# Block 0's x^T handed over on the chip, and the way from projection into attention rearranged

## The chip, the cores and the metric

One core of a Trainium2 chip runs the program. The metric is the time of one execution in microseconds (us) of device time; three executions of the kernel before gave 1452.94, 1455.36 and 1454.16 us, median 1454.16. A smaller time is better.

## The reference

One transformer block over 2048 tokens of width 512, all in fp32:

```python
xn = _layernorm(x, axis=-1)          # x: 1 x 2048 x 512
s = _A_ref(xn, A_wqkv, A_wo)         # 32 heads of 16: softmax(q k^T / 4) v, then @ wo
g = _silu(_B_ref(xn, B_w_gate, B_w_up, B_w_down))   # (silu(xn wg) * (xn wu)) wd, 1792 hidden
return x + s * g
```

Attention and the feed-forward network (FFN) read the same normalised x, and meet only in the last line.

## The kernel before, in words

Numbers keep their precision by being split: a value is held as a rounded high part and the rest as a low part, and a product is three matmuls (high-high, low-high, high-low). The program has two stages.

**Projection.** Tokens go in four blocks of 512 (loop `b`, L650), and each block in twelve slots (loop `n`, L654). A slot makes one tile of 128x512 with twelve matmuls (`project`, L568): eight feature tiles (q and k, `feature_tile`, L612) and four value tiles (`value_tile`, L624). Block 0 has the value tiles first, the others last. The order of everything is written out by hand: what a slot issues stands in the loop body, each engine takes its instructions in that order, and so do the queues of SyncE (SP) and GpSimd (POOL), which issue the DMAs.

- In slots 8 to 10 the next block's x is transposed on TensorE into PSUM and split by `turn_x` (L552) into `xt[b % 2]`, two tiles of 128 x 4 x 512: ScalarE casts the high part (L558), VectorE subtracts for the low part (L561). GpSimd then stores both to DRAM, in `xt_d` (L562 to L564). `load_fx` (L147) brings them back in the FFN's layout, `fx`: 64 contraction rows, once in each half of the partitions, so that two matmuls can use the two halves of the array. The loads for block 0 are issued at slot 5 of blocks 1 and 2 (L662).
- A feature tile is split into `parts` by ScalarE (L617) and VectorE (L619) and stored by SP (L621); ScalarE squares it into `sq` (L618). `parts` comes from a pool of three buffers (`p3`), `sq` from one of five (`p5`); the `ps` tiles in PSUM have four.
- `squares` (L584) sums the squares of each head, by a matmul with a 0/1 matrix, into 32 partitions of a PSUM bank: tiles 0 to 3 in `bankx`, tiles 4 to 7 in `banky`, four matmuls side by side. `add` (L641) does this for whatever is pending, as soon as four are (L688) and at `flush` (L645), which takes the maximum over tokens.
- In block 3, the maxima over all blocks give one number `s4`, an upper bound of the scores (L708 to L719), and from it `flag`: 1 where a fixed shift is safe. `fill(3 * DC)` (L720) puts the first 24 steps of the FFN between slots 9 and 10. After slot 10's tile two matmuls with one row (L723, L724) spread `s4` over partitions and 512 columns, and ScalarE writes the shift from there (L725, to be stored in `sh_d` by GpSimd) and into the first query tile (L728).
- At slot 8 of block 3 SP issues attention's first loads: `load_k` for two tiles (twelve DMAs), `load_q` (six) and `load_v` (two).

**The handover.** `nc.values_load(flag)` (L733) reads the flag into a register of each engine; `tc.If(fast < 1)` (L734) holds a general way that this input does not take, so each engine branches across it. The last value tile's store is issued behind it (L766).

**Attention and FFN.** Loop over 32 units (L791) of eight steps: four score matmuls, ScalarE's exponential of 128x1024 (L805), value matmuls (L367). `share` (L451) puts a planned number of FFN steps into each step, so that TensorE always has work.

Of the kernel before, what the change touches and what calls it, by code (L numbers as in the profile page):

```python
# [13 lines left out]
AF = mybir.ActivationFunctionType  # L14
# [11 lines left out]
NB = 4  # L26
TB = S // NB
NT = TB // P
DT = D // P
KT = S // P  # L30
NG = H // 4
# [5 lines left out]
HALF = 64  # L37
# [13 lines left out]
def tile_block(ctx: ExitStack, tc: tile.TileContext, x, wqkv, wo, w_gate, w_up, w_down, out):  # L51
# [51 lines left out]
    def load_k(g, c, i=None):  # L103
        load_rows(kst[(g * NB + c) % RING if i is None else i],
                  k_d[:, g * 64:(g + 1) * 64, c * TB:(c + 1) * TB], KSLOT)

    def load_q(u, i=None):
        g, b = divmod(u, NB)
        load_rows(qst[u % 2 if i is None else i], q_d[:, g * 64:(g + 1) * 64, b * TB:(b + 1) * TB], QSLOT)
# [37 lines left out]
    def load_fx(b, j):  # L147
        for h in range(2):
            dst = fx[h * HALF:(h + 1) * HALF, j].bitcast(F32).rearrange("p (c u) t -> u p c t", u=2)
            for u in range(2):  # L150
                sp.dma_start(dst[u], xt_d[b, j, u * HALF:(u + 1) * HALF])
# [304 lines left out]
    with ExitStack() as pro:  # L456
        pc = pro.enter_context(tc.tile_pool(name="pc", bufs=1))
        p2 = pro.enter_context(tc.tile_pool(name="p2", bufs=2))
        p3 = pro.enter_context(tc.tile_pool(name="p3", bufs=3))
        p5 = pro.enter_context(tc.tile_pool(name="p5", bufs=5))  # L460
        plast = pro.enter_context(tc.tile_pool(name="plast", bufs=1))
        pps = pro.enter_context(tc.tile_pool(name="pps", bufs=4, space=PSUM))

# [88 lines left out]
        def turn_x(b, t, between=None):  # L552
            a = acc[t % 2]
            for c in range(DT):
                nc.tensor.transpose(a[:, c * P:(c + 1) * P], xn[t][:, c * P:(c + 1) * P], ident)
            hi, lo = (xt[b % 2][j][:, :, t * P:(t + 1) * P] for j in range(2))
            av = a.rearrange("p (c f) -> p c f", f=P)
            nc.scalar.copy(hi, av)  # L558
            if between:
                between()  # L560
            dve.tensor_sub(lo, av, hi.bitcast(F32))  # L561
            if t == NT - 1:  # L562
                for j in range(2):
                    pool.dma_start(xt_d[b, j], xt[b % 2][j].bitcast(F32))  # L564

# [46 lines left out]
        def feature_tile(b, m):  # L612
            xh, xl = xt[b % 2]
            ps = project([(wh[:, m, c], wl[:, m, c], c) for c in range(DT)], xh, xl, None)
            parts = p3.tile([P, 2, TB], F32R, tag="parts", name="parts")
            sq = p5.tile([P, TB], BF, tag="sq", name="sq")
            nc.scalar.copy(parts[:, 0], ps)  # L617
            act(sq, ps, AF.Square)  # L618
            dve.tensor_sub(parts[:, 1], ps, parts[:, 0].bitcast(F32))  # L619
            dst = (q_d if m < 4 else k_d)[:, (m % 4) * P:(m % 4 + 1) * P, b * TB:(b + 1) * TB]  # L620
            sp.dma_start(dst.rearrange("s f t -> f s t"), parts.bitcast(F32))  # L621
            return m, sq

        def value_tile(b, t):  # L624
            xh, xl = xt[b % 2]
            order = then = None
            if b == 0:
                parts = (slice(0, 2), slice(2, 3)) if t == 0 else (slice(0, 3, 2), slice(1, 2))
                order = [(i, part) for part in parts for i in range(DT)]
                then = partial(turn_x, 0, 1, partial(later, 3)) if t == 0 else None  # L630
            ps = project([(vh[:, c], vl[:, c], c) for c in range(DT)], xh, xl, slice(t * P, (t + 1) * P), order, then)
            nc.scalar.copy(vt5[:, :, t, :, :DH], ps.rearrange("p (g h d) -> p g h d", g=NG, h=4))
            if t == NT - 1:
                store = partial((pool if b < NB - 1 else sp).dma_start, v_d[:, :, b * NT:(b + 1) * NT].rearrange("g p t c -> p g t c"), vt)
                if b < NB - 1:
                    store()
                return store

        pend = []

        def add():  # L641
            while pend:
                squares(*pend.pop(0))
# [6 lines left out]
        for b in range(NB):  # L650
            more = b + 1 < NB
            slots = [(feature_tile, m) for m in range(8)]
            slots = [(value_tile, t) for t in range(NT)] + slots if b == 0 else slots + [(value_tile, t) for t in range(NT)]
            for n, (make, i) in enumerate(slots):  # L654
                if b == 0:
                    if n + 5 < 12:
                        load_w(worder[n + 5])
                    if n >= 2 and n + 2 < 12:
                        split_w(worder[n + 2], pool)
                if n == (1 if b else 2) and more:  # L660
                    load_x(b + 1)
                if b in (1, 2) and n == 5:  # L662
                    load_fx(0, b - 1)
                if b == 2 and n in (6, 7):
                    load_gu(n - 6)
                if b == 2 and n == 8:
                    load_wd(0)
                if not more and n == 2:
                    split_gu(0)
                    for bank in acc:  # L670
                        dve.memset(bank, 0.0)
                if b == NB - 1 and n == 8:
                    for c in range(2):
                        load_k(0, c)
                    load_q(0)
                    for c in range(2):
                        load_v(0, c)
                if b == 0 and n == 1:
                    rates(2, NT)
                    norm(2)  # L680
                    norm(3)
                made = make(b, i)
                if b == 0 and n == 1:
                    for t in (2, 3):
                        turn_x(0, t)
                if n == 0 and b == 1:
                    flush(0)
                elif len(pend) == 4:  # L688
                    add()
                if make is feature_tile:  # L690
                    pend.append(made)
                if b == 0 and n == 11:
                    ring(0, 2, one)
                    queries(0, one)
                if more:
                    if 2 <= n < 6:
                        stats(n - 2)
                    if n == 5:
                        rates(0, NT)
                    if 6 <= n < 10:  # L700
                        norm(n - 6)
                    if 8 <= n < 11:
                        turn_x(b + 1, n - 8)
                    if n == 10:
                        turn_x(b + 1, NT - 1)
                if n == 8 and b:
                    flush(b)
                if not more and n == 8:  # L708
                    dve.reduce_max(pk, peak, axis=AX.X)
                    dve.tensor_add(sm, pk[:, 0:1], pk[:, 1:2])  # L710
                if not more and n == 9:
                    tops = pps.tile([P, 512], F32, tag="ps", name="tops")
                    nc.tensor.transpose(tops[0:1, :P], sm, ident)
                    dve.reduce_max(s4, tops[0:1, :P], axis=AX.X)
                    dve.tensor_scalar(s4, s4, 0.51, None, op0=ALU.mult)
                    dve.tensor_scalar(flag, s4, LIMIT, None, op0=ALU.is_le)
                    dve.tensor_scalar(sel[:, :NG * NB], row[:, :NG * NB], s4, None, op0=ALU.mult)
                    for h in range(2):
                        dve.tensor_copy(selq[:, h * HALF:h * HALF + 1], s4)  # L719
                    fill(3 * DC)  # L720
                if not more and n == 10:
                    low, high = [pps.tile([P, 512], F32, tag="ps", name="low") for _ in range(2)]
                    mm(high[:2 * NG * NB], sel, row, start=True, stop=True, skip_group_check=True)  # L723
                    mm(low[:HALF + 2], selq, row, start=True, stop=True, skip_group_check=True)  # L724
                    act(shift, high[:2 * NG * NB], AF.Copy, scale=-1.0)  # L725
                    for h in range(2):
                        two_rows = slice(h * HALF, h * HALF + 2)
                        act(qst[0][two_rows], low[two_rows, None, :].to_broadcast([2, 2, 512]), AF.Copy, scale=-1.0)  # L728
                    for j in range(4):
                        pool.dma_start(sh_d[:, j * 512:(j + 1) * 512], shift.bitcast(F32))  # L730


        fast = nc.values_load(flag, min_val=0, max_val=1)  # L733
        with tc.If(fast < 1):  # L734
            with tc.tile_pool(name="gen", bufs=1) as gen:
                for h in range(2):
# [160 lines left out]
```

## Time and profile before

| what | value |
|---|---|
| median of three executions | 1454.16 us (1452.94 to 1455.36) |
| the profiled execution's own time | 1451.71 us |
| its span, first to last instruction | 1449.9 us |
| granted TensorE clock, mean | 0.998 |
| TensorE busy | 1433.2 us, 99% |
| ScalarE busy | 1094.4 us, 75% |
| VectorE busy | 539.9 us, 37% |
| first score matmul of attention | at 166.50 us |

The projection stage ends at about 165 us, so all that the change touches lies in the first ninth of the span. PE is TensorE's matmuls, PEld its weight loads, DVE VectorE, ACT ScalarE; a q behind the name (PEldq, SPq) means the engine's instruction queue, where register loads, branches and DMA issues are recorded. "x <- y" in a wait means that x stood idle until y was done.

### The profile page before, as it was taken

How to read it: one execution, taken by the hardware profiler on the slowest of the kernel's cores; microseconds unless marked ns; L12 is line 12 of the kernel's file. 1: busy time of each engine (PE TensorE's matmuls, PEld its weight loads, DVE VectorE, ACT ScalarE, POOL GpSimd, SP SyncE). 2: the span in 40 equal slices, each digit the busy share in tenths (PEclk: the TensorE clock that was granted, in tenths of full speed). 3: DMA queues.
4: the chain of work that ended last, by engine and by line, in shares of the span. 5: the costliest groups of instructions: out<-in, count | busy, mean ns of one | idle time of the engine just before them, and what ended most of it. 6: DMA issues, size and time to landing. Idle time of an engine off the chain costs nothing.

```text
span 1449.9 us, 26818 instructions
## 1 busy us (share of the span) xinstructions
PE 1433.2 (99%) x11237; PEld 804.1 (55%) x11237; DVE 539.9 (37%) x905; ACT 1094.4 (75%) x1219; POOL 89.9 (6%) x105
## 2 busy tenths in 40 slices
PE   8999999999999999999999999999999999999997
PEld 7777555555555555555555555555555555555554
DVE  6543343313423343143324431343243412424445
ACT  4433588878888888788888887888888877887774
POOL 4200200000000000000000000000000000000153
PEclk9999999999999999999999999999999999999999
DMA  8899652033264420143634311345425202315252
GB/s 267 271 288 290 160 125 71 19 76 76 66 155 105 109 71 27 40 110 78 134 75 120 87 41 34 78 102 111 122 63 125 60 21 51 78 41 169 75 205 78
DMA packets 129556, 154.92 MB, mean 107 GB/s; under 512 B 12700, under 2 KB 79260, under 8 KB 128404
## 3 DMA queue, kind: packets, MB, share of 16 engines
q1 hardware_dynamic: 123940, 130.38, 35.3%
q0 software_dynamic: 5200, 22.22, 4.0%
q8 instruction: 91, 1.49, 0.5%
q10 hardware_dynamic: 288, 0.52, 0.1%
q14 instruction: 37, 0.30, 0.1%
HBM read 111.13 MB, written 41.94 MB: 106 GB/s over the span
## 4 chain that ended last, share of the span: by engine, by line
PE 86%; ACT 2%; DVE 1%; issue 0%; DVEq 0%; ACTq 0%
PE acc L367 32%; PE bankx L174 30%; PE score L803 20%; PE banky L174 3%; ACT pr L805 2%; PE bankx L330 0%; DVE y L854 0%; DVE y L857 0%; DVE rl L839 0%; PE score L863 0%; DVE fx L242 0%; DVE y L179 0%; DVEq L893 0%; ACT th L178 0%; DVE fx L241 0%
## 5 line engine op out<-in xcount | busy, mean ns | idle before, releaser
L805 ACT ACTIVATE pr<-score 128x1024 f32<-128x1024 f32 x1024 | 992.3, 1023 | 234.0 <-PE score L803 233.4
L367 PE MATMUL acc<-pr,vst 128*17 128x512 f32 x4096 | 489.2, 595 | 0.0
L803 PE MATMUL score<-qst,kst 50*128 50x512 f32 x2048 | 354.8, 422 | 4.0 <-ACT pr L805 2.4
L803 PEld LDWEIGHTS score<-qst,kst 50*128 50x128 f32 x2048 | 177.3, 184 | 268.9 <-ACT pr L805 229.2
L174 PE MATMUL bankx<-fx,guh 64*128 64x512 f32 x896 | 288.6, 392 | 0.0
L174 PE MATMUL banky<-fx,guh 64*128 64x512 f32 x896 | 288.5, 392 | 0.0
L367 PEld LDWEIGHTS acc<-pr,vst 128*17 128x17 f32 x4096 | 93.9, 96 | 235.9 <-issue 235.0
L204 DVE SCALAR_TENSOR_TENSOR ga<-th,bankx 128x512 f32<-128x512 f32 x56 | 38.5, 688 | 461.2 <-ACT th L203 461.2
L174 PEld LDWEIGHTS bankx<-fx,guh 64*128 64x128 f32 x896 | 165.7, 185 | 34.3 <-issue 0.4
L174 PE MATMUL banky<-fx,gul 64*128 64x512 f32 x448 | 175.4, 392 | 0.0
L174 PE MATMUL bankx<-fx,gul 64*128 64x512 f32 x448 | 175.3, 391 | 0.0
L174 PEld LDWEIGHTS banky<-fx,guh 64*128 64x128 f32 x896 | 165.7, 185 | 2.7
L174 PE MATMUL banky<-wd,hh 64*128 64x512 f32 x672 | 165.4, 388 | 0.0
L174 PE MATMUL bankx<-wd,hh 64*128 64x512 f32 x672 | 165.4, 388 | 0.0
L174 PEld LDWEIGHTS bankx<-wd,hh 64*128 64x128 f32 x672 | 124.0, 184 | 25.6
L174 PEld LDWEIGHTS banky<-wd,hh 64*128 64x128 f32 x672 | 124.0, 184 | 1.4
L174 PEld LDWEIGHTS bankx<-fx,gul 64*128 64x128 f32 x448 | 82.9, 185 | 17.9
L174 PEld LDWEIGHTS banky<-fx,gul 64*128 64x128 f32 x448 | 82.8, 185 | 1.4
L578 PE MATMUL ps<-xt,wh 128*128 128x512 f32 x256 | 81.0, 397 | 0.0
L135 DVE TENSOR_TENSOR gul<-gur,guh 128x1024 fp32r<-128x1024 f32 x56 | 68.6, 1225 | 2.1
L222 DVE COPY facc<-bankx 128x512 f32<-128x512 f32 x16 | 11.1, 692 | 153.0 <-PE banky L174 140.1
L390 POOL DMA_DIRECT2D o_d<-o x12 | 7.5, 623 | 825.6 <-DVE o L388 825.6
(146 smaller groups left out, 1052.7 us busy)
## 6 DMA issues: line engine op xcount, KB each, us to landing
fx<-xt_d SPq DMA_DIRECT2D x32, 512.0 KB
gur<-in_B_w_gate_dram SPq DMA_DIRECT2D x56, 256.0 KB
gur<-in_B_w_up_dram SPq DMA_DIRECT2D x56, 256.0 KB
wdr<-in_B_w_down_dram SPq DMA_DIRECT2D x56, 256.0 KB
kst<-k_d SPq DMA_DIRECT2D x192, 64.0 KB
qst<-q_d SPq DMA_DIRECT2D x192, 64.0 KB
xt_d<-xt POOLq DMA_DIRECT2D x8, 1024.0 KB, 8.5
q_d<-parts SPq DMA_DIRECT2D x16, 512.0 KB
```

What stands on the lines that cost most here:

```text
L135: dve.tensor_sub(lo, raw, hi.bitcast(F32))
L174: mm(bank, lhs[h], rhs[h], start=start, stop=stop)
L204: dve.scalar_tensor_tensor(ga, th, 1.0, bankx, op0=ALU.add, op1=ALU.mult)
L222: dve.tensor_copy(facc[:, t], bankx)
L367: mm(a[h * 32:h * 32 + DH + 1], v[:, kt % CT, h * (DH + 1):(h + 1) * (DH + 1)], probs[2 * i + h // 2][:, h % 2], start=kt == 0, stop=kt == ...
L390: (pool if g < NG - 1 else sp).dma_start(o_d[g // 2, b], o2)
L578: mm(ps, w, a[:, c], start=n == 0, stop=n == 3 * DT - 1)
L803: mm(score[j][:, h], k[r, j, kc * P:(kc + 1) * P], q[r, j], start=True, stop=True)
L805: exps.append(act(pr, score[j], AF.Exp, scale=0.25))
```

## The change

It has five parts.

1. Block 0's x^T is no longer stored to DRAM and loaded again. ScalarE copies it from `xt[0]` into `fx` with sixteen copies of 64 partitions x 1024 elements (`copy_fx`), one per slot from slot 3 of block 0 to slot 6 of block 1, behind the slot's tile.
2. The squares are summed once per block, eight at a time, at `flush`; `sq` has nine buffers. ScalarE squares a tile before it copies it, and `parts` has four buffers.
3. The two matmuls that spread `s4` have 8 columns in place of 512, and ScalarE broadcasts the first column to 512.
4. Attention's first loads are issued over slots 1, 3, 5 and 6 of block 3 in place of slot 8.
5. The flag is read behind slot 10 of block 3, ahead of the last tile.

Line numbers of the kernel after are seven higher from L713 on (L803 is L810), and the scalar square and copy change places in L617 and L618.

```diff
-        p3 = pro.enter_context(tc.tile_pool(name="p3", bufs=3))
-        p5 = pro.enter_context(tc.tile_pool(name="p5", bufs=5))
+        p3 = pro.enter_context(tc.tile_pool(name="p3", bufs=4))
+        p5 = pro.enter_context(tc.tile_pool(name="p5", bufs=9))
...
-            if t == NT - 1:
+            if t == NT - 1 and b:
                 for j in range(2):
                     pool.dma_start(xt_d[b, j], xt[b % 2][j].bitcast(F32))
...
+            act(sq, ps, AF.Square)
             nc.scalar.copy(parts[:, 0], ps)
-            act(sq, ps, AF.Square)
...
+        def copy_fx(i):
+            i, w = divmod(i, 2)
+            i, u = divmod(i, 2)
+            j, h = divmod(i, 2)
+            dst = fx[halves[h], j].rearrange("p (c u) t -> u p c t", u=2)[u]
+            nc.scalar.copy(dst[:, 2 * w:2 * w + 2], xt[0][j][halves[u], 2 * w:2 * w + 2])
...
-                if b in (1, 2) and n == 5:
-                    load_fx(0, b - 1)
...
-                if b == NB - 1 and n == 8:
-                    for c in range(2):
-                        load_k(0, c)
+                if not more and n in (1, 3):
+                    load_k(0, n // 2)
+                if not more and n == 5:
                     load_q(0)
+                if not more and n == 6:
                     for c in range(2):
                         load_v(0, c)
...
+                if b < 2 and 0 <= 12 * b + n - 3 < 16:
+                    copy_fx(12 * b + n - 3)
                 if n == 0 and b == 1:
                     flush(0)
-                elif len(pend) == 4:
-                    add()
...
-                    mm(high[:2 * NG * NB], sel, row, start=True, stop=True, skip_group_check=True)
-                    mm(low[:HALF + 2], selq, row, start=True, stop=True, skip_group_check=True)
-                    act(shift, high[:2 * NG * NB], AF.Copy, scale=-1.0)
+                    mm(high[:2 * NG * NB, :8], sel, row[:, :8], start=True, stop=True, skip_group_check=True)
+                    mm(low[:HALF + 2, :8], selq, row[:, :8], start=True, stop=True, skip_group_check=True)
+                    act(shift, high[:2 * NG * NB, 0:1].to_broadcast([2 * NG * NB, 512]), AF.Copy, scale=-1.0)
                     for h in range(2):
                         two_rows = slice(h * HALF, h * HALF + 2)
-                        act(qst[0][two_rows], low[two_rows, None, :].to_broadcast([2, 2, 512]), AF.Copy, scale=-1.0)
+                        act(qst[0][two_rows], low[two_rows, None, 0:1].to_broadcast([2, 2, 512]), AF.Copy, scale=-1.0)
                     for j in range(4):
                         pool.dma_start(sh_d[:, j * 512:(j + 1) * 512], shift.bitcast(F32))
-
-
-        fast = nc.values_load(flag, min_val=0, max_val=1)
+                    fast = nc.values_load(flag, min_val=0, max_val=1)
```

## The prediction, on record before the result

> **What bounds the kernel now.** I read the page first: the busy times, then the chain of work that ended last.
>
> ```profile
> PE 1433.2 (99%) x11237; PEld 804.1 (55%) x11237; DVE 539.9 (37%) x905; ACT 1094.4 (75%) x1219; POOL 89.9 (6%) x105
> ...
> PE   8999999999999999999999999999999999999997
> ...
> PE 86%; ACT 2%; DVE 1%; issue 0%; DVEq 0%; ACTq 0%
> ```
>
> TensorE (PE) is busy in 1433.2 of 1449.9 us and carries 86% of the chain. It takes its instructions in order, so the change is worth what it takes from, or adds to, PE's own queue: fewer matmuls, or fewer gaps. The change touches only the stage ahead of attention, so I cut that stage into stretches of 5 us (columns: length, then busy time and instructions of PE, PEld, DVE, ACT, POOL, then granted clock, DMA share, GB/s).
>
> ```profile
> 135.00:140.00 5.00, 4.04 (x17) 3.07 (x17) 1.39 (x2) 2.64 (x6) 0.00 (x0) 1.00 0.76 281
> 160.00:165.00 5.00, 4.89 (x16) 2.39 (x15) 0.00 (x0) 3.22 (x5) 2.10 (x4) 1.00 0.85 192
> 165.00:170.00 5.00, 3.09 (x22) 2.42 (x24) 0.00 (x0) 3.23 (x4) 0.00 (x0) 1.00 0.75 252
> ```
>
> From the second slice of the page on (36 us) PE is full but for two gaps: one of 0.96 us after 135, and one of most of 2 us after 165, where projection hands over to attention. The waits name them:
>
> ```profile
> ACT parts L617 <- DMA q_d<-parts: 12.6, 5, 4.6
> PE bankx L585 <- ACT sq L618: 1.0, 1, 1.0
> PE score L803 <- PEq L734: 1.6, 1, 1.6
> ```
>
> The first gap is a square that came late from ScalarE (ACT), which itself had stood behind a copy waiting for a `parts` buffer still being stored. The second is PE's own sequencer at the branch of the `If`. Since PE stays full afterwards, I take a microsecond won here as a microsecond off the end.
>
> **Part 1: the late square goes.** PE around the first gap, and ACT:
>
> ```profile
> 134.59 0.40 PE L585 MATMUL bankx<-sq,ind 128*32 128x512 bf16 x3
> 135.96 0.38 PE L585 MATMUL bankx<-sq,ind 128*32 128x512 bf16 x1 [0.97 <-ACT sq L618]
> 136.26 0.73 PE L578 MATMUL ps<-xt,wh 128*128 128x512 f32 x2
> ```
>
> ```profile
> 134.82 0.59 ACT L617 CAST parts<-ps 128x512 fp32r<-128x512 f32 x1 [4.57 <-DMA q_d<-parts]
> ```
>
> An undisturbed batch of four squares looks like this:
>
> ```profile
> 49.65 0.62 PE L578 MATMUL ps<-xt,wh 128*128 128x512 f32 x2
> 50.11 0.40 PE L578 MATMUL ps<-xt,wl 128*128 128x512 f32 x1
> 50.44 0.40 PE L585 MATMUL banky<-sq,ind 128*32 128x512 bf16 x4
> 50.77 0.74 PE L578 MATMUL ps<-xt,wh 128*128 128x512 f32 x2
> ```
>
> From the first square to the next projection: 136.26 - 134.59 = 1.67 us against 50.77 - 50.44 = 0.33, so the wait costs **1.34 us**. In the changed kernel the square is issued ahead of the copy, so it no longer waits for the buffer; `parts` has four buffers; and the batch is taken four slots later, behind eleven us of projection. If that cover went (ACT four slots late), the wait would return at its 1.34. The DMA traffic that held the buffer also shrinks:
>
> ```profile
> fx<-xt_d SPq DMA_DIRECT2D x32, 512.0 KB
> xt_d<-xt POOLq DMA_DIRECT2D x8, 1024.0 KB, 8.5
> ```
>
> Block 0 is one of four: 2 of the 8 stores (2 MB) and 8 of the 32 loads (4 MB) go, off GpSimd's queue and SP's. They save PE nothing further, since it had no other gap there.
>
> **Part 2: squares in eights.** Two matmuls of projection take 50.11 - 49.65 = 0.46 us, one 0.23, so in the undisturbed case PE was free for the squares at 50.11 + 0.23 = 50.34 and the batch costs 50.77 - 50.34 = 0.43. Eight batches of four become four of eight. No batch of eight is in the trace. Its bounds: 0.43 (the second four hidden wholly) and 0.86 (nothing shared). The four run side by side in 0.40, so I add one 0.23 stream to 0.43: 0.66, a saving of 0.2 each. Four times: **0.8 us**, bounds 0 and 1.7.
>
> **Part 3: sixteen copies on ACT.** What ACT does in a slot of block 0, and what a copy of 1024 elements costs:
>
> ```profile
> 25.91 0.59 ACT L617 CAST parts<-ps 128x512 fp32r<-128x512 f32 x1 [1.69 <-PE ps L578]
> 26.40 0.60 ACT L618 ACTIVATE sq<-ps 128x512 bf16<-128x512 f32 x1
> 26.89 0.62 ACT L497 CAST wh<-wraw 128x512 fp32r<-128x512 f32 x1
> 28.71 0.59 ACT L617 CAST parts<-ps 128x512 fp32r<-128x512 f32 x1 [1.21 <-PE ps L578]
> ```
>
> ```profile
> 167.28 5.61 ACT L805 ACTIVATE pr<-score 128x1024 f32<-128x1024 f32 x6 [1.77 <-PE score L803]
> ```
>
> Operations of 512 elements follow each other in 0.49 us, those of 1024 in 5.61/6 = 0.93 or a little less. A slot lasts 28.71 - 25.91 = 2.80 and holds three of 0.49: 1.47, leaving 1.33. A copy at 0.93 fits; ACT stays behind PE by less than a slot and the `ps` buffers, four of them, hide it. The cover is thin at one place: the change from block 0 to block 1, where the projection needs all of block 1's x^T, and a copy (of slot 10) now stands ahead of the last two casts:
>
> ```profile
> 45.05 1.08 ACT L558 CAST xt<-acc 128x512 fp32r<-128x512 f32 x2
> ```
>
> ```profile
> 45.80 1.28 DVE L561 TENSOR_TENSOR xt<-acc,xt 128x512 fp32r<-128x512 f32 x2
> ```
>
> ```profile
> 47.55 0.64 PE L578 MATMUL ps<-xt,wh 128*128 128x512 f32 x2
> ```
>
> Now VectorE ends at 45.80 + 1.28 = 47.08, and the second matmul of the new block, which reads its result, starts at 47.55 + 0.23 = 47.78: 0.70 of room. The copy takes 0.93: **+0.3 us** with the signal's time. Bounds: 0 and +1.0 (no room at all). In block 1 the copies end with slot 6, before the next casts.
>
> **Part 4: from the small matmuls to the first score.** PE, then ACT:
>
> ```profile
> 159.83 1.07 PE L723 MATMUL low<-row,sel 1*64 1x512 f32 x2
> 160.83 1.07 PE L724 MATMUL low<-row,selq 1*66 1x512 f32 x2
> 161.83 0.73 PE L580 MATMUL ps<-vh,xt 128*128 128x512 f32 x2
> 164.50 0.40 PE L580 MATMUL ps<-vl,xt 128*128 128x512 f32 x1
> 166.50 0.73 PE L803 MATMUL score<-qst,kst 50*128 50x512 f32 x3 [1.61 <-PEq L734]
> ```
>
> ```profile
> 164.93 0.59 ACT L632 COPY vt<-ps 128x512 f32<-128x512 f32 x1 [0.93 <-PE ps L580]
> ```
>
> From L723 to the first score: 166.50 - 159.83 = 6.67. The two matmuls are 2.00 of it; with 8 columns in place of 512 I put them at 0.35 (nothing like them is in the trace; bounds 0 and 2.00). But their time may not come through, for the branch has its own clock. The flag's load and the branch, by engine's queue:
>
> ```profile
> L733 PEldq TENSOR_LOAD <-flag x1: 486/486/486, 159.9 to 159.9; - x1
> ```
>
> ```profile
> L734 SPq EVENT_SEMAPHORE  x8: 17/17/17, 164.5 to 165.1; - x8
> L734 DVEq COMPARE_BRANCH  x1: 72/72/72, 159.0 to 159.0; - x1
> L734 PEldq COMPARE_BRANCH  x1: 5158/5158/5158, 160.4 to 160.4; - x1
> L734 SPq COMPARE_BRANCH  x1: 50/50/50, 161.2 to 161.2; - x1
> L734 DVEq EVENT_SEMAPHORE  x1: 21/21/21, 162.6 to 162.6; - x1
> ```
>
> PE's sequencer runs ahead: it read the flag at 159.9, as L723 started, with tile 11 still queued. So the load's 0.49 is hidden from the matmuls already, but it holds up the branch (160.4), which ends at 160.4 + 5.16 = 165.6; 0.9 of semaphores later comes the first score. Read ahead of tile 11, the load is off that path: the branch starts about 0.6 earlier against L723, and the load itself lies under tile 10, whose 24 loads and matmuls are queued ahead. On ACT, VectorE and GpSimd the moved load holds back nothing that is due: ACT's last copy waits for tile 11 anyway.
>
> How long will the branch take? VectorE went on 162.6 - 159.0 = 3.6 us after its branch and SP 164.5 - 161.2 = 3.3; PE's 5.2 fell into the stretch with a DMA share of 0.85, behind these weight loads:
>
> ```profile
> 159.43 0.63 SPq L127 DMA_DIRECT2D gur<-in_B_w_up_dram  x1
> ```
>
> With the attention loads moved to slots 1 to 6, SP reaches them some ten us earlier (twelve K and six Q loads no longer stand ahead), so I take 3.75, near the two other engines. Then the first score stands at 0.02 + 3.75 + 0.9 = 4.67 after the first small matmul: a gain of **2.0 us**. Bounds: with 5.16 again, 6.08, a gain of 0.6. At best the branch hides entirely; then tile 11 (164.90 - 161.83 = 3.07), its copy (0.59) and the signals (0.3) follow the 0.35: 4.3, a gain of 2.4. That copy binds because the score tiles reuse the projection's PSUM.
>
> [...]
>
> The loads themselves: SP issues the same number, earlier, between the stores; two slots then hold six extra issues each, and the fourth `parts` buffer hides a store that is late by a slot. Cost 0.
>
> **Sum.** -1.34 - 0.8 + 0.3 - 2.0 = **-3.8 us**. Against the profiled execution's 1451.71 us (span 1449.9) that is 1447.9; its time is 2.45 under the median of the runs shown, so against the median of 1454.16 I say **1450.3 us**.
>
> **Rivals.**
>
> *The branch keeps its 5.16 us.* For: nothing says that the DMA load made it longer, and SP's branch fell in the same stretch with 3.3. Against: it is the longest of the three and the traffic moves away. Then part 4 is 0.6 and the sum -2.4: 1451.7 us. Chance 0.27; this falls within 0.2%.
>
> *ACT becomes the bound in block 0* (the other side). The copies go from SBUF to SBUF across halves of the partitions, a form the trace does not hold; nearest is the weight cast at 0.62 for 512 against 0.59 from PSUM, which speaks against. Should a copy hold ACT for 2.5 us, it exceeds what a slot leaves by 2.5 - 1.33 = 1.17 in each of slots 4 to 10 (the last three hold a fourth operation, but are longer by their transposes): 8.2 us that PE meets at block 1, and the sum is +4.4: 1458.5 us. Above 1.33 ACT falls behind; from 1.33 + 3.8/7 = 1.9 the whole change loses. Chance 0.06.
>
> *Nothing but the late square goes* (eights cost as two fours, the branch as before, the room at block 1 lost): -1.34 + 0.3 - 0.6 = -1.6, 1452.5 us. Chance 0.10, within 0.2%.
>
> **How the numbers follow.** 0.2% of the time, 2.9 us, is about what a measurement can tell from no change. The forecast with its own spread (-2.9 to -5) holds 0.57; the first and third rival 0.37, nearly all within 0.2%; the ACT rival 0.06. So faster 0.60, same 0.34, slower 0.06. The range takes in the bounds of part 2 and part 4 and the first and third rival, and leaves out the ACT rival and the extremes together: 1448.6 to 1453.2.
>
> **What would show it.** In the changed profile: no wait of L585 for ACT; four batches of eight squares of about 0.66; ACT copies to `fx` at 0.93 apart; a PE gap of 0.3 at the start of block 1's first tile; the two small matmuls under 0.5 together; from the first of them to the first score 4.7 us; PE's branch near 3.7. I am wrong if PE's branch stays above 5, if PE waits for ACT in block 0 or 1, or if PE has new gaps after the handover.

## The result and the profile after

The kernel after takes **1448.20 us** (median of seven executions, 1448.02 to 1450.87), the kernel before 1453.76 (seven, among them the three of the start, 1452.94 to 1455.36). The ratio is 0.9964, with a 95% interval of 0.9953 to 0.9976: faster by 0.36%. The prediction was 1450.3 with a range down to 1448.6, so the time lies 0.4 us below the range.

The two profiled executions, however, differ by what the sum said: 1451.71 us before, 1448.02 after (span 1446.2, clock 0.998), which is -3.69 against a sum of -3.8. Two lines of the page after, its busy times and the shares of the chain that ended last:

```profile
PE 1430.6 (99%) x11237; PEld 804.3 (56%) x11237; DVE 538.9 (37%) x905; ACT 1110.2 (77%) x1235; POOL 88.7 (6%) x103
...
PE 96%; ACT 2%; DVE 1%; issue 0%; DMA 0%; DVEq 0%; ACTq 0%
```

PE has the same 11237 matmuls in 2.6 us less; ACT has sixteen operations and 15.8 us more and still stands at 77%. PE carries 96% of the chain, where it was 86%. The stretches of 5 us that the prediction showed, now after (columns as there):

```profile
135.00:140.00 5.00, 5.00 (x23) 4.05 (x22) 1.38 (x2) 1.60 (x4) 0.00 (x0) 1.00 0.91 148
160.00:165.00 5.00, 3.86 (x23) 2.60 (x21) 0.00 (x0) 3.36 (x5) 1.55 (x3) 1.00 0.79 227
165.00:170.00 5.00, 4.32 (x34) 1.94 (x36) 0.84 (x1) 3.97 (x6) 0.82 (x1) 1.00 0.32 109
```

After 135 PE is now full (5.00 of 5.00, before 4.04): the late square is gone. The gap at the handover moved from the stretch after 165 into the one after 160, because the handover comes earlier. The waits of PE name two that bear on the change:

```profile
PE score L810 <- ACT vt L632: 1.0, 1, 1.0
...
PE acc L555 <- DVE xt L561: 0.3, 1, 0.3
```

The handover, PE (columns: start, length, engine, line, operation, what ended the idle time before it):

```profile
157.97 0.28 PE L730 MATMUL low<-row,sel 1*64 1x8 f32 x2
158.18 0.28 PE L731 MATMUL low<-row,selq 1*66 1x8 f32 x2
158.39 0.73 PE L580 MATMUL ps<-vh,xt 128*128 128x512 f32 x2
...
161.06 0.40 PE L580 MATMUL ps<-vl,xt 128*128 128x512 f32 x1
162.47 0.97 PE L810 MATMUL score<-qst,kst 50*128 50x512 f32 x4 [1.01 <-ACT vt L632]
```

The first small matmul starts at 157.97 (before 159.83) and the first score at 162.47 (before 166.50): -1.86 by then, -4.03 in all. These 4.03 are not the 3.7 by which the span is shorter: PE's last matmul still comes 4.0 earlier (1439.12, before 1443.08), and 0.3 is lost behind it, where the output is stored. The two small matmuls take 158.39 - 157.97 = 0.42, and from the first of them to the score it is 4.50 us in place of 6.67. The branch, by each engine's queue, and ACT's last copy:

```profile
L741 DVEq COMPARE_BRANCH  x1: 72/72/72, 157.2 to 157.2; - x1
L741 PEldq COMPARE_BRANCH  x1: 3729/3729/3729, 158.0 to 158.0; - x1
L741 DVEq EVENT_SEMAPHORE  x1: 21/21/21, 160.1 to 160.1; - x1
```

```profile
161.49 0.58 ACT L632 COPY vt<-ps 128x512 f32<-128x512 f32 x1 [0.40 <-PE ps L580]
```

PE's branch starts with the first small matmul and takes 3.73 us (before 5.16), VectorE goes on 160.1 - 157.2 = 2.9 us after its own (before 3.6). PE's branch ends at 158.0 + 3.73 = 161.73, ACT's copy at 161.49 + 0.58 = 162.07. The view names the copy, the later of the two, as the end of PE's wait. The score starts 0.40 behind it and 0.74 behind the branch; in k1_again below, where the branch is over long before, a score starts 0.09 behind that copy. So it is the branch that binds here, and the copy would bind some 0.3 us earlier.

What then makes the medians differ by 5.56 and not by 3.69? That is the question for the experiments.

### The profile page after: what moved, and what is told of

It is laid out like the page before. It is cut to its first block, busy times and chain, and to the rows that moved or that the text cites. A ratio compares the mean times of both kernels' runs of the same rounds, so it can differ in the third digit from the quotient of the medians.

```text
span 1446.2 us, 26820 instructions
## 1 busy us (share of the span) xinstructions
PE 1430.6 (99%) x11237; PEld 804.3 (56%) x11237; DVE 538.9 (37%) x905; ACT 1110.2 (77%) x1235; POOL 88.7 (6%) x103
## 4 chain that ended last, share of the span: by engine, by line
PE 96%; ACT 2%; DVE 1%; issue 0%; DMA 0%; DVEq 0%; ACTq 0%
PE acc L367 32%; PE bankx L174 30%; PE score L810 20%; PE ps L578 6%; PE banky L174 4%; PE ps L580 3%; ACT pr L812 2%; PE acc L555 0%; PE bankx L330 0%; DMA facc<-in_A_x_dram 0%; DVE y L861 0%; DVE xn L550 0%; ACT xt L558 0%; DVE y L864 0%; PE bankx L585 0%
## 5 line engine op out<-in xcount | busy, mean ns | idle before, releaser
L810 PE MATMUL score<-qst,kst 50*128 50x512 f32 x2048 | 355.1, 422 | 3.4 <-ACT pr L812 2.4
L810 PEld LDWEIGHTS score<-qst,kst 50*128 50x128 f32 x2048 | 177.5, 185 | 268.4 <-ACT pr L812 230.6
```

Of the source, the lines that this page charges most:

```text
L810: mm(score[j][:, h], k[r, j, kc * P:(kc + 1) * P], q[r, j], start=True, stop=True)
```

## The experiments

**Theory** (mine, Theory A): the kernel before loses TensorE's clock in most of its executions. After the handover with its two matmuls of one row (2.0 us) and its gap of 1.6 us, the granted clock falls for a few microseconds. The profiled execution of before is one of the few in which it did not fall (its clock is 1.00 in the stretches after 160 and 165 that the prediction shows), so it is 2.45 us under the median; the kernel after has less of what makes the clock fall, and its profiled execution lies 0.18 under its median. **Rival**: the rest of the difference is scatter of the executions or of the chip, and returns to 3.7 elsewhere. For the parts of the change, each experiment has its own question.

All kernels start from the kernel after; each was timed beside the kernel before on its chip. The kernel before: 1455.13 in the first group (k0_after to k3_flag), 1453.30 in the second (k6_cover to k5_fours), 1452.92 in the third. The clock is the mean granted TensorE clock of an execution.

**k0_after**: the kernel after, unchanged, on another chip.

> The changed kernel once more. Open: the two profiled executions differ by 3.7 us (1451.71 and 1448.02), the medians by 5.6 (1453.76 and 1448.20). Theory A (the clock): the unprofiled executions of before are longer because TensorE is granted less clock in them. Then the executions of before lie near a clock of 0.996 to 0.997 with spans of 1451 to 1453, those of the changed kernel near 0.998 to 0.999 with 1446 to 1447; at an equal clock the spans differ by 3.7. Theory B (the handover): the branch of before takes a varying time, and the profiled execution caught a short one. Then the clocks are alike and spans of before are 1.5 to 2 us longer than 1449.9 at 0.998.

Measured: 1448.21 us (1447.95 to 1448.36), ratio 0.9951 (0.9937 to 0.9964); clock 0.998 to 0.999, beside 0.995 to 0.997 for before. The kernel before is 1.4 us slower on this chip, the kernel after is not. The difference grows to 6.9 and does not return to 3.7 (on the third chip, k0_again below, it is 5.0): against the rival.

**k1_cols**: the two small matmuls with 512 columns again.

```diff
-                    mm(high[:2 * NG * NB, :8], sel, row[:, :8], ...)
-                    mm(low[:HALF + 2, :8], selq, row[:, :8], ...)
-                    act(shift, high[:2 * NG * NB, 0:1].to_broadcast([2 * NG * NB, 512]), ...)
+                    mm(high[:2 * NG * NB], sel, row, ...)
+                    mm(low[:HALF + 2], selq, row, ...)
+                    act(shift, high[:2 * NG * NB], ...)
```

> The changed kernel with 512 columns again in the two small matmuls. Mine (they stand on the path once the branch is short): they take 2.0 us instead of 0.42, tile 11 and its copy end 1.6 later, the first score follows 1.4 to 1.6 us later than in the changed kernel, and so does the end: +0.1%. Rival (the branch has its own clock and hides them): the first score stays within 0.3 us.

Measured: 1450.75 us (1449.48 to 1451.61), 0.9967 (0.9955 to 0.9979); clock 0.996 to 0.998. That is 2.5 over k0_after, not the 1.6 by which the matmuls are longer (2.00 against 0.42). Stretches of 2 us, and PE in them:

```profile
155.00:160.00 5.00, 5.00 (x25) 2.94 (x21) 1.37 (x2) 1.18 (x2) 0.00 (x0) 1.00 0.05 10
160.00:162.00 2.00, 2.00 (x8) 1.01 (x8) 0.00 (x0) 1.53 (x2) 1.06 (x3) 1.00 0.01 4
162.00:164.00 2.00, 2.00 (x7) 1.53 (x6) 0.00 (x0) 1.08 (x2) 1.04 (x3) 0.54 0.87 199
164.00:166.00 2.00, 1.44 (x4) 0.62 (x2) 0.00 (x0) 0.52 (x1) 0.00 (x0) 0.61 0.20 72
```

```profile
158.95 1.07 PE L730 MATMUL low<-row,sel 1*64 1x512 f32 x2
159.95 1.07 PE L731 MATMUL low<-row,selq 1*66 1x512 f32 x2
...
161.51 0.40 PE L580 MATMUL ps<-vl,xt 128*128 128x512 f32 x1
...
162.25 0.63 PE L580 MATMUL ps<-vl,xt 128*128 128x512 f32 x1
```

The column behind POOL is the clock. PE is busy without a pause from 155 to 164, and yet the clock falls to 0.54 and 0.61 behind the two one-row matmuls; a matmul then takes 0.63 in place of 0.40. The loss is 2 x 0.46 + 2 x 0.39 = 1.70 us of clock: at half speed (0.50 stands in a whole stretch of k2_loads, below) that is 3.4 us, an estimate. So there is a fall at this place, as Theory A has it. It is not the only loss in this profile, which is the slowest of the six executions (clock 0.996): its first small matmul starts at 158.95, that of k1_again (below), the same kernel, at 157.99, so 0.96 us are lost ahead of all that the edit touches.

**k2_loads**: attention's loads at slot 8 again.

```diff
-                if not more and n in (1, 3):
-                    load_k(0, n // 2)
...
+                if b == NB - 1 and n == 8:
+                    for c in range(2):
+                        load_k(0, c)
+                    load_q(0)
+                    for c in range(2):
+                        load_v(0, c)
```

> The changed kernel with attention's first loads at slot 8 again. Mine (the branch's length hangs on the DMA traffic that these loads and the weight loads behind them make): PE's branch takes 5 us again instead of 3.7, and the end comes 1.2 to 1.5 us later. Rival (the branch takes 3.7 as soon as the flag is read early, whatever the traffic): within 0.3 us.

Measured: 1450.91 us (1449.43 to 1451.16), 0.9969 (0.9956 to 0.9981); clock 0.997 to 0.998; 2.7 over k0_after. PE's branch by its queue, then the score behind it on PE, then a stretch of 2 us behind that (the lines are one lower here):

```profile
L740 PEldq COMPARE_BRANCH  x1: 5829/5829/5829, 158.1 to 158.1; - x1
```

```profile
164.79 0.93 PE L809 MATMUL score<-qst,kst 50*128 50x512 f32 x4 [3.22 <-PEq L740]
```

```profile
166.00:168.00 2.00, 2.00 (x12) 1.72 (x11) 0.00 (x0) 1.52 (x2) 0.00 (x0) 0.50 0.94 323
```

With the short matmuls and the early flag in place, only the loads' place stretches the branch from 3.73 to 5.83. PE then stands for 3.2 us, and the clock falls to 0.50 behind it. While the branch lasts, the DMA engines move 204 GB/s in the kernel before and 68 in the kernel after; here they move 226 and 152 in the two stretches of 2 us from 160 to 164. The rate alone does not set the length: in k1_cols it is 4 in the stretch after 160, in k7_full, below, 72 and 186 in those after 162 and 164, and the branch takes 3.59 and 3.65. What is shown is that it hangs on these loads; the rival of the prediction, that it keeps its 5.16, falls.

**k3_flag**: the flag read directly ahead of the branch.

```diff
-                    fast = nc.values_load(flag, min_val=0, max_val=1)
...
+        fast = nc.values_load(flag, min_val=0, max_val=1)
         with tc.If(fast < 1):
```

> The changed kernel with the flag read behind tile 11 again. Mine: the load of 0.49 us stands ahead of PE's branch again, which starts 0.6 later and ends 0.6 later; the first score comes 0.5 to 0.6 later, the end too. Rival (the copy of tile 11 binds, not the branch): within 0.2 us.

Measured: 1448.89 us (1448.39 to 1450.09), 0.9956 (0.9942 to 0.9969); clock 0.997 to 0.999; 0.7 over k0_after. PE's branch by its queue, then PE from the first small matmul to the score, then a stretch of 2 us behind that:

```profile
L741 PEldq COMPARE_BRANCH  x1: 3618/3618/3618, 158.9 to 158.9; - x1
```

```profile
158.28 0.28 PE L730 MATMUL low<-row,sel 1*64 1x8 f32 x2
...
163.31 0.93 PE L810 MATMUL score<-qst,kst 50*128 50x512 f32 x4 [1.55 <-PEq L741]
```

```profile
166.00:168.00 2.00, 2.00 (x13) 1.47 (x10) 0.00 (x0) 1.54 (x3) 0.00 (x0) 0.52 0.42 135
```

The first small matmul stands at 158.28 here, so the branch starts 0.6 behind it and the score 5.03 behind it (after: 4.50). That is the 0.5 that the early flag is worth. The clock fell behind a gap of 1.55 us in this execution, to 0.52 in this stretch; the kernel after has one of 1.01, and kept 1.00.

**k7_full**: nine useless matmuls of 128 rows (they write a PSUM tile that the small ones overwrite) ahead of the short small ones: PE's 2 us again, but with all rows. If the length of the detour takes the clock, it falls here too; if the single row does, it doesn't.

```diff
+                    for _ in range(9):
+                        mm(high, wh[:, 0, 0], xt[1][0][:, 0], start=True, stop=True, ...)
                     mm(high[:2 * NG * NB, :8], sel, row[:, :8], ...)
```

> The changed kernel with nine useless matmuls of 128 rows and 512 columns (2.1 us) right ahead of the two small ones: as long on TensorE as the 512 columns with one row of the kernel before, but with all rows at work. Theory A (the clock falls behind a stretch in which few rows work, whether TensorE counts as busy or not): the clock stays at 0.998 to 0.999, the time is that of the changed kernel and 1.4 to 1.6 us, 1449.7. Rival (the clock falls for the gap at the branch alone, and the 512 columns have no part in it but their time): the clock and the time are those of the kernel with 512 columns, 0.996 to 0.998 and 1450.75.

Measured: 1450.19 us (1449.63 to 1450.96, eleven executions), 0.9981 (0.9972 to 0.999); clock 0.998 to 0.999 in all eleven. PE, and then the two stretches in which k1_cols lost its clock:

```profile
158.94 2.25 PE L731 MATMUL low<-xt,wh 128*128 128x512 f32 x9
161.12 0.28 PE L732 MATMUL low<-row,sel 1*64 1x8 f32 x2
```

```profile
162.00:164.00 2.00, 2.00 (x11) 1.60 (x10) 0.00 (x0) 1.95 (x3) 1.68 (x4) 1.00 0.33 72
164.00:166.00 2.00, 1.00 (x6) 0.55 (x6) 0.00 (x0) 0.58 (x1) 0.42 (x1) 1.00 0.78 186
```

The nine cost 161.12 - 158.94 = 2.18 on PE, and the kernel is 2.0 slower than after: their own time and nothing more. The clock stays at 1.00. So the fall goes with the single row and not with the delay. It goes with it in some executions only: a clock of 0.997 or less is found in 8 of the 17 of k1_cols and k1_again, in none of these eleven. The three groups ran on three chips, so a part of the chip in this is not excluded.

**k6_cover**: an attempt to close the gap that is left. The small matmuls, the shift and the flag go ahead of slot 10's tile, and three of the FFN's steps stand right behind the branch, taken from the first share.

```diff
+AHEAD = 3
...
-        shares[0] -= FIRST
+        shares[0] -= FIRST + AHEAD
...
-                if not more and n == 10:
...
         made()
+        fill(AHEAD)
```

> The changed kernel with the two small matmuls, the shift and the flag's read moved ahead of slot 10's tile, and three of the FFN's steps moved from attention's first step to the place right behind the branch. Mine (branch and copy are what is left of the handover): PE's branch starts some 3.7 us ahead of tile 11's end and is over with it; the three steps (0.7 us) cover the copy; TensorE has no gap over 0.3 us, the end comes 0.6 to 0.9 earlier than in the changed kernel, and the clock is 0.998 to 0.999 in every execution, since no quiet stretch is left there. Rival (the wait moves to the exponentials, which come 0.2 later): within 0.2 us of the changed kernel.

Measured: 1448.75 us (1448.54 to 1449.41), 0.997 (0.9957 to 0.9982); clock 0.997 to 0.998: not faster than after. The gap is closed (the first score at 162.22, FFN in front of it), but attention's first steps now lack the FFN steps:

```profile
164.83 0.50 PE L810 MATMUL score<-qst,kst 50*128 50x512 f32 x2 [0.42 <-ACT pr L812]
165.75 0.49 PE L810 MATMUL score<-qst,kst 50*128 50x512 f32 x2 [0.41 <-ACT pr L812]
166.67 0.80 PE L810 MATMUL score<-qst,kst 50*128 50x512 f32 x2 [0.42 <-ACT pr L812]
```

```profile
168.00:170.00 2.00, 2.00 (x16) 0.34 (x8) 1.97 (x3) 0.58 (x1) 1.94 (x2) 0.50 0.76 143
```

The first fence is PE, the second a stretch of 2 us. Three short gaps, and the clock falls in the third score pair (0.80 for 0.49), to 0.50 in the stretch after 168. My expectation failed. That the steps were taken from the wrong place is tried in k8_best.

**k4_dram**: block 0 through DRAM again, the other parts kept.

```diff
-            if t == NT - 1 and b:
+            if t == NT - 1:
...
+                if b in (1, 2) and n == 5:
+                    load_fx(0, b - 1)
...
-                if b < 2 and 0 <= 12 * b + n - 3 < 16:
-                    copy_fx(12 * b + n - 3)
```

> The changed kernel with block 0's x^T through DRAM again (no copies on ScalarE). Mine (the copies cost TensorE 0.3 us at the end of block 0, and the traffic that they spare hid nothing): between 0.4 earlier and 0.1 later than the changed kernel. Rival (the 6 MB of traffic held the buffers of parts, and with them the squares): a wait of over 0.5 us for ScalarE is back and the end comes 0.5 to 1.3 later.

Measured: 1447.97 us (1446.81 to 1448.36), 0.9962 (0.9948 to 0.9975); clock 0.997 to 0.999. Two executions at 0.999 took 1446.81 and 1447.10, below anything that the kernel after gave, but the median is not clearly apart from it: this leaves the question open (k4_again below).

**k5_fours**: the squares in fours again, the copy ahead of the square, three `parts` and five `sq` buffers; the copies to `fx` stay.

```diff
+                elif len(pend) == 4:
+                    add()
...
-            act(sq, ps, AF.Square)
             nc.scalar.copy(parts[:, 0], ps)
+            act(sq, ps, AF.Square)
```

> The changed kernel with the squares in fours, behind the copy, and three and five buffers again. Mine: eight batches of 0.43 us in place of four of 0.64, so 0.9 us later; the late square does not come back, since the traffic that held the buffers is gone. Rival (buffers and order removed the late square): 2.2 us later, with a wait of L585 for ScalarE of 1 us in block 3.

Measured: 1448.97 us (1448.20 to 1450.06, ten executions), 0.9967 (0.9958 to 0.9977); clock 0.997 to 0.999; 0.7 to 1.0 over the kernel after (1447.91 to 1448.21 in the groups beside it). PE's wait of L585 for ACT did not come back, though the buffers and the order are those of before. But the reason that I had given for it is wrong. ACT's copies still wait for stores, nearly as long in all as in the kernel before (there 12.6 us in total, 5 times, the longest 4.6):

```profile
ACT parts L617 <- DMA q_d<-parts: 11.9, 5, 3.4
```

In the kernel after and in k4_dram ACT has no such wait. So it is the order and the buffers that end ACT's waits, and not the spared traffic. Here the waits only fall elsewhere: the copies at 138.97 and 143.47 wait now, the one ahead of the batch at 135.45 does not. This kernel also keeps attention's loads at their new slots, so whether those or block 0's spared traffic moved the waits is open. The 0.8 or so is about the price of fours (0.84 by the rows below).

**k0_again** and **k4_again**: the kernel after and k4_dram once more, side by side.

> The changed kernel once more, beside the three that follow on one chip. Expected: 1448.2 us, as twice before, clock mostly 0.998 to 0.999.

> The changed kernel with block 0's x^T through DRAM again, beside the changed kernel on the same chip. At a clock of 0.999 it took 1446.8 and 1447.1 us on another chip, the changed kernel 1448.0 to 1448.2. Mine (the copies on ScalarE cost TensorE a wait at the end of block 0, 0.5 us in all, and are the one part of the change that loses): 0.5 to 1.1 us earlier at the same clock. Rival (that was the chip): within 0.2 us.

Measured: k0_again 1447.91 us (1447.72 to 1449.06), 0.9967 (0.9955 to 0.9979); k4_again **1447.08** (1446.87 to 1448.02), 0.9961 (0.9948 to 0.9975); clock 0.998 to 0.999 in both. Without the copies it is 0.8 faster. PE in k4_again:

```profile
43.33 1.03 PE L555 MATMUL acc<-ident,xn 128*128 128x128 f32 x8
44.12 0.72 PE L578 MATMUL ps<-xt,wh 128*128 128x512 f32 x2
...
161.83 0.94 PE L810 MATMUL score<-qst,kst 50*128 50x512 f32 x4 [0.99 <-ACT vt L632]
```

The eight transposes of slot 10 go in one run, and the next projection starts 44.12 - 43.33 = 0.79 behind their first; in the kernel after (rows below) it is 44.66 - 43.34 = 1.32. Of the 0.6 us by which the score is earlier than in the kernel after (162.47), 0.53 are this.

**k8_best**: k4 and k6 together, with the three FFN steps taken from the third share in place of the first.

```diff
+        shares[2] -= AHEAD
```

> The same with the small matmuls and the flag ahead of slot 10's tile and three FFN steps behind the branch, which are taken from the third share and not from the first, so that attention's first step keeps its own. Mine (without the cover in that step TensorE went quiet there and the clock fell): the clock stays at 0.998 to 0.999 and the end comes 0.6 to 1.0 us ahead of the kernel before this one. Rival (the clock falls all the same, since the exponentials bound the first steps): 0.996 to 0.997 and no gain.

Measured: **1446.63 us** (1446.50 to 1447.69), 0.9959 (0.9945 to 0.9973); clock 0.999, in one execution 0.998. This is the best version: 6.3 under before on its chip and 1.3 under k0_again, 0.45 under k4_again. The clock is as expected, which agrees with the cause given for the miss of k6_cover; the gain is smaller than the 0.6 to 1.0 that I had said. PE at the handover:

```profile
160.28 0.40 PE L582 MATMUL ps<-vl,xt 128*128 128x512 f32 x1
160.83 0.47 PE L175 MATMUL bankx<-fx,guh 64*128 64x512 f32 x1
...
161.62 0.72 PE L811 MATMUL score<-qst,kst 50*128 50x512 f32 x4
```

The FFN's steps begin 160.83 - 160.28 - 0.40 = 0.15 us behind the last tile, and the first score follows them without a gap.

**k1_again**: k1_cols on the third chip.

> The changed kernel with 512 columns in the small matmuls, beside the changed kernel on the same chip. Theory A (the clock): 2.0 to 2.6 us later than the changed kernel, of which 1.5 is the matmuls' own time, with a clock of 0.996 to 0.998 where the changed kernel has 0.998 to 0.999. Rival (the matmuls' time alone): 1.5 us later at the same clock.

Measured: 1450.13 us (1449.04 to 1450.82, eleven executions), 0.998 (0.9971 to 0.9989). They lie on two levels: five at 1449.04 to 1449.35 with a clock of 0.998 or 0.999, six at 1450.13 to 1450.82 with 0.997 or 0.998. The lower level is 1.3 over k0_again, the matmuls' own time; the upper is 1.1 to 1.8 above the lower, about one fall of the clock. Its profiled execution was one of the lower level, without a fall in the handover: one profile of such a kernel can show the loss or not. PE's branch by its queue, PE, and ACT:

```profile
L741 PEldq COMPARE_BRANCH  x1: 3429/3429/3429, 158.0 to 158.0; - x1
```

```profile
163.77 0.99 PE L810 MATMUL score<-qst,kst 50*128 50x512 f32 x4 [0.72 <-ACT vt L632]
```

```profile
163.09 0.59 ACT L632 COPY vt<-ps 128x512 f32<-128x512 f32 x1 [0.93 <-PE ps L580]
```

The branch starts with the first long matmul and is over at 158.0 + 3.43 = 161.43; the copy ends at 163.09 + 0.59 = 163.68, and the score follows 0.09 behind it. With long matmuls it is the copy that binds.

## Why the prediction was right and wrong

**The step that failed** is the last of the sum: "its time is 2.45 under the median of the runs shown, so against the median of 1454.16 I say 1450.3 us". I carried the distance between the profiled execution and the median over as a constant. It is a term of its own, and the change acts on it. The 48 executions of the kernel before in the three groups and the 18 of the kernel after (the result's, k0_after, k0_again), by their clock, with the mean of their times:

| clock | before: executions, us | after: executions, us |
|---|---|---|
| 0.999 | 5, 1451.74 | 9, 1447.99 |
| 0.998 | 7, 1451.98 | 6, 1448.32 |
| 0.997 | 18, 1453.43 | 2, 1448.82 |
| 0.996 | 11, 1454.86 | 1, 1450.87 |
| 0.995 | 7, 1456.20 | none |

At the same clock of 0.999 or 0.998 the difference is 3.75 or 3.66, which is the sum. The other 1.9 us of the 5.6 between the medians (before's median over all 48 is 1453.64, and 1453.64 - 1451.74 = 1.9) are executions at a lower clock: 36 of 48 before, 3 of 18 after. One fall of 1.70 us is 1.70 / 1446 = 0.0012 of the clock, so a step of the table is roughly one fall, and its 1.4 us agree. It is no exact count, since the mean takes in a fall behind PE's last matmul too, as in both profiles (0.50 after 1446 before, after 1442 in the kernel after). k1_cols puts falls back with one-row matmuls, k7_full shows that the same time with full rows takes none, k2_loads and k3_flag show them behind gaps of 3.2 and 1.55 us.

That the falls of the kernel before are these is argued and not shown. Its one profile has none until PE's last matmul is done, and no execution of it with a low clock was profiled. The two places that the traces show are also too few for its slowest executions: 1456.20 - 1451.74 = 4.5 us is some three falls, and the places are one in the handover or right behind it (k1_cols, k2_loads, k3_flag, k6_cover) and one between 8 and 14 us. The early one stands in the profile of k4_dram (0.77, 0.50 and 0.88 in the stretches of 2 us from 8 to 14), ahead of all that the change and the edit touch, so it does not come from this change. The profiles of k1_cols and k7_full come to the handover 0.96 and 0.97 us late (158.95 against 157.99 in k1_again; 158.94, the first of the nine matmuls, against 157.97 in the kernel after), which such a fall would explain. Where a third lies is open.

So the range should have let this term vary between 0.2 and 2.45, which alone moves its lower end to 1447.9 + 0.2 = 1448.1. That the sum of -3.8 meets the -3.69 of the two profiles so well is in part luck: by the rows it is -4.03 at the first score, of which 0.3 is lost at the end of the program.

**Part 1 of the prediction, the late square: -1.34, right in size, half right in its cause.** I gave it several cures. Order, buffers and the later batch are enough without the spared traffic (k4_dram, k4_again: PE doesn't wait, and ACT waits for no store). The spared traffic is not a cure of its own: without the others ACT's waits for stores stay (k5_fours), and PE escapes them by where they fall.

**Part 2, eights: -0.8, right.** The batch in the kernel after, with the transposes that part 3 speaks of:

```profile
43.34 0.60 PE L555 MATMUL acc<-ident,xn 128*128 128x128 f32 x4
44.26 0.66 PE L555 MATMUL acc<-ident,xn 128*128 128x128 f32 x4 [0.32 <-DVE xt L561]
44.66 0.70 PE L578 MATMUL ps<-xt,wh 128*128 128x512 f32 x2
...
47.54 0.64 PE L578 MATMUL ps<-xt,wh 128*128 128x512 f32 x2
...
50.10 0.40 PE L578 MATMUL ps<-xt,wl 128*128 128x512 f32 x1
50.43 0.40 PE L585 MATMUL bankx<-sq,ind 128*32 128x512 bf16 x4
50.66 0.39 PE L585 MATMUL banky<-sq,ind 128*32 128x512 bf16 x4
50.98 0.73 PE L578 MATMUL ps<-xt,wh 128*128 128x512 f32 x2
```

PE is free at 50.10 + 0.23 = 50.33 and goes on at 50.98: 0.65, where I had 0.66. Four times, against 8 x 0.43: -0.84.

**Part 3, the copies: +0.3 in the sum, 0.5 to 0.8 measured, and at another place.** I had looked for the gap at block 1's first tile; at 47.54 there is none. It is one slot earlier, inside the transposes of slot 10: the second four wait at 44.26 for VectorE's subtraction, which waits for ACT's cast, which now stands behind a copy. In k5_fours, where ACT squares behind the copy again, most of the loss is where I had looked: the matmuls of block 1's first tile start at 48.00 and 48.86, 0.86 apart in place of 0.46. So the mechanism was right, the size too small and the place a matter of ACT's order. ACT's copies:

```profile
26.87 1.05 ACT L645 CAST fx<-xt 64x1024 fp32r<-64x1024 f32 x1
27.82 0.62 ACT L497 CAST wh<-wraw 128x512 fp32r<-128x512 f32 x1
```

The next operation starts 0.95 later, where I had 0.93, so the rival of a copy of 2.5 us falls. By k4_again the sixteen copies of `copy_fx` cost 0.8 on the median and bring nothing, as long as the other parts stand. The three terms up to the small matmuls make -1.34 - 0.84 + 0.53 = -1.65 by these rows, where -1.86 was measured; 0.2 us is left without a place.

**Part 4, the handover: -2.0, measured 4.50 - 6.67 = -2.17, right by its mechanism.** The branch took 3.73 (I had 3.75) and starts with the first small matmul; the small matmuls 0.42 (0.35). The score follows the branch's end by 0.74, where I had 0.9. The bound that I had named for the best case, ACT's copy of the last tile, lies only 0.3 us below that. The branch takes 3.4 to 3.7 us in ten profiles with attention's loads moved, 5.2 and 5.8 in the two with the loads at slot 8; what PE waits for in that time no run here shows. The smaller matmuls did not shorten it: with long ones it takes 3.43 and 3.59 (k1_again, k1_cols) and starts with the first of them all the same. What they bring is that the last tile and ACT's copy of it end earlier, so that the copy no longer binds: from the first small matmul to the score it is 163.77 - 157.99 = 5.78 in k1_again, 4.50 here.

**The chances.** Faster by over 0.2%, to which I gave 0.60, is what came; the cases within 0.2% counted on a branch of 5.16, which k2_loads shows to belong to the loads' old place.

## What to carry to other kernels

A sum made against one profiled execution predicts the difference of two such executions, not of the medians: first compare the profiled clock and time with the list of all executions, and where the profile is one of the best, ask what the others lose and whether the change touches it. PE's branch over skipped code took 3.4 to 3.7 us here, and 5.2 or 5.8 with bulk loads beside it, so move such loads away from it and start it early. When an engine with spare time gets work, look for its cost where something else waits for that engine in order, not in its share of busy time.

## What the runs showed of the hardware

The clock fell to half for about 3.4 us at a time. This length is an estimate from two measured numbers: the clock is 0.50 in whole stretches of 2 us (k2_loads 166 to 168, k4_dram 10 to 12, k6_cover 168 to 170), and with the stretches beside them a fall takes 1.70 us of clock in k1_cols, k2_loads, k3_flag and k4_dram, 1.72 in k6_cover. On what comes ahead of a fall the runs differ: the clock fell behind a gap of 3.22 us (k2_loads) and of 1.55 us (k3_flag), behind three of 0.41 to 0.42 us (k6_cover), and in k1_cols behind 2 us of matmuls with one row, with PE busy all the time from 155 to 164. By k7_full, matmuls with 128 rows in their place keep it, 1.00 in the same stretches. The same gap or the same rows do not bring a fall each time: the kernel before (2.0 us of one-row matmuls, then a gap of 1.61 us) and k1_again kept 1.00 in their profiles. What makes one gap bring a fall and another not was not measured.
